# A block mask in an attention and mixer kernel: twelve wide matmuls and comparisons become one small group, one comparison and nine GpSimd copies, and the written order is new

## The chip, the cores and the metric

The kernel runs on one core of one Trainium2 chip. The core has five engines that work beside each other, each in its own order: TensorE (PE in the profile, its weight loads PEld), VectorE (DVE), ScalarE (ACT), GpSimd (POOL) and SyncE (SP), which here only issues DMAs. Each engine takes its instructions strictly in turn: one that waits holds up all behind it on that engine. The metric is the device time of one execution in microseconds (us), the median of three runs.

## The reference, cut to what matters

Attention with a block mask, and a mixer behind it. Batch 4, 8 heads, 768 tokens, 64 channels a head; the mask is made of blocks of 32 by 32, so 24 by 24 flags.

```python
scores = (1 / sqrt(64)) * q @ k.T
mask = |bi - bj| <= 1, or bi or bj in (0, 23), or bj in sampled_blocks[bi]   # bi, bj: block of row, column
attn = softmax(where(mask, scores, -1e9));  x = (attn @ v), heads side by side: [4, 768, 512]
u = x + (x.T @ U @ V).T                     # U [768, 32], V [32, 768]
out = u + relu(u @ w_ch1) @ w_ch2           # w_ch1 [512, 2048], w_ch2 [2048, 512]
```

## The kernel before

**Tiling.** The work on heads goes by pairs of heads: 16 pairs, four to a batch (`HP = 4`). A token is stored at partition p and position t as token 6p + t, so a tile of 128 partitions and 6 positions holds the 768 tokens, and a block of 32 tokens is a short stretch of partitions at each position. Scores are held transposed, keys on partitions, queries along the row; the exponential is taken without a maximum; the row of ones in `vts` makes the product with v give the sum too.

**Two ways to mask.** In the pairs 0 to 3 the mask sits in the matmul: beside the 64 channels of a head stand 24 rows, one-hot block numbers with the queries and block biases (0 or -240) with the keys, so that masked scores vanish in the exponential. From pair 4 on the queries and keys hold channels alone, two heads on the two halves of the array, and the exponentials are multiplied on VectorE by a tile `mask` of zeros and ones, 128 partitions by 6 key groups by 768 queries (`half_quad`, L990; the product is L1016). That tile has to be made once, before the first of these products. `mask_part` (L908) makes it: for each of 6 key groups and 2 halves of the queries one matmul of 24 meaningful rows (`kmask`, a zeroed tile into which a DMA, L197, copies the bias rows of the keys) against the one-hot rows, giving the bias of 128 keys for 384 queries, and one comparison on VectorE (L916) that turns it into zeros and ones.

**Steps and the written order.** A long string, `PLAN` (L436), lists the steps; each word is one step, and TensorE, VectorE, ScalarE and SyncE execute in the order in which the words issue their instructions. GpSimd isn't under that order: a scheduler of the framework places its instructions, by when it reckons them ready. A digit behind a word is the bank of PSUM (eight, numbered 0 to 7) that the step takes first. The words that matter here:

- `S` a score step of one key group in pairs 0 to 3, two matmuls of 384 columns; `B` one of two key groups, four matmuls, 1536 columns in three banks; `e` the exponential of the oldest score step not yet taken, on ScalarE. The 8 heads of pairs 0 to 3 have 48 key groups: here 30 `S` and 9 `B`, counted below as scores #1 to #48.
- `A` the product with v of one key group (6 matmuls of 65 columns), `v` the division on VectorE (L532, L539), `M`, `D`, `X`, `Y`, `E` steps of the low-rank mixer of pairs 0 to 3, with `m`, `d`, `y`, `g` their VectorE parts.
- `R` turns one half (queries or keys) of the next pair by six TensorE transposes (`turn_qk`, L921), and `t` copies it from PSUM on VectorE. `Z`, `z` do so for the second head of pair 0.
- `K` one `mask_part`, and `k` its comparison.
- `Q` a score step of both heads of a pair for two key groups (from pair 4 on; eight matmuls, L1001), `H` without dots one head of it; each gives two, or one, `e` of 1536 elements and as many `p`, the products with the mask. Below, Q4 is the first `Q` of pair 4, and so on. `V` is the product with v of one head.
- `U`, `P`, `C` and `a.`, `b`, `a` are the first mixer matmul and its relu, `H.`, `S.`, `D.` the second one in a scheme of seven products in place of eight, and `g.`, `h.` and what belongs to them the same for the last batch.

**Loads.** Queries, keys and values of pair i are loaded as float32 by SyncE (`load_qk`, `load_v`, L145 to L165), and cast to float16 on GpSimd (L139 for pairs up to 5). The load tiles and the cast tiles are doubled; the queue of SyncE stops at a load whose tile hasn't been cast away. `load_mix` (L199) brings U and V, cast on GpSimd too (L205, L206).

Of the kernel before, what the change touches and what calls it, by code (L numbers as in the profile page):

```python
# [19 lines left out]
P = 128  # L20
# [3 lines left out]
def kernel(  # L24
# [93 lines left out]
    kmask = consts.tile([P, S], FP16, name="kmask")  # L118
# [71 lines left out]
    for tile_ in (qres[1], kres[1], Vt, kmask):  # L190
        nc.gpsimd.memset(tile_.bitcast(FP32), 0.0)

    def second_set():
        for h in range(2):
            one_hot(1, h)
            nc.sync.dma_start(out=kres[1][mrows[h], h, :], in_=kres[0][mrows[h], h, :])
        nc.sync.dma_start(out=kmask[mrows[0], :], in_=kres[0][mrows[0], 0, :])  # L197
# [239 lines left out]
    S0 S3 e e S5 B0 e Z7 e S3 z Z6 e z B0 A7 A e R6 S3 t A R5 e A B0 t A K6 e A S3 k v A5 A e K6 k B0 A  # L437
    A e K7 A K6 k S3 k A K7 e v B0 k S3 e M6 e A5 A m R7 A t B0 K6 R3 e k A A t S6 A e v S0 D2 S3 e d A7
    A e A S0 K6 A e S3 k K2 A e S5 k A e v S3 R2 e S5 t S0 e M7 e S3 m D2 e B5 d A0 D1 e A A d A S3 D2 A
    e d K1 S5 k R7 e S3 t A S1 e v A5 A e A S3 S6 e K2 A e A k A S3 v B0 e K7 M6 e k S3 m X5 K7 e A6 Y k  # L440
    A B0 y X7 Y e S3 y E5 A e A g A R7 S0 t A e v S4 S2 e A7 A e R1 E6 A t A g A A Q v e e M6 X7 m Y P6
    y p H U7 e p H b C e p H b U7 e p H b U6 e p E1 a g p V7 Q v e e V6 U7 v p U0 a P1 b C p P6 a C E7 Q
    a g U6 e e U7 b P6 b p U0 C a U7 p a Q b X6 Y e e P7 y C P6 b C p U0 b a p V7 L.5 Q v U.0.1.3.6 e
    q.3.0 V7 a.0.1.3.0 e U.0.1.1.1 v U.0.1.11.0 a.0.1.1.1 U.0.1.5.6 q.3.1 a.0.1.11.1 p Q a.0.1.5.1 p
    U.0.1.10.6 e U.0.1.7.7 a.0.1.10.0 e U.0.1.2.6 a.0.1.7.0 S.0.0.1.3 U.0.1.9.7 p a.0.1.2.1 Q a.0.1.9.1
    q.7.1 U.0.1.4.6 e S.0.0.2.0 H.0.0.1.0.7 p H.0.0.1.1 a.0.1.4.1 U.0.1.0.0 p L.6 e U.0.1.14.1 q.4.1 V6
    a.0.1.0.1 p a.0.1.14.1 Q v q.4.0 e V6 D.0.0.0 S.0.0.3 H.0.0.6.0 e v U.0.1.13.2 q.7.0 H.0.0.6.1
    U.0.1.12.6 a.0.1.13.1 D.0.0.2 y p Q a.0.1.12.1 q.5.1 H.0.0.7.0 e H.0.0.7.1 q.5.0 H.0.0.5.0.6 D.0.0.3
    H.0.0.5.1 e S.0.0.4.4 U.0.1.6.1 p H.0.0.4.0 a.0.1.6.1 H.0.0.4.1 D.0.0.4 Q D.0.0.5 p H.0.0.3.0 e L.7
    H.0.0.3.1 p H.0.0.2.0.7 H.0.0.2.1 e p U.0.1.8.2 U.0.1.15.0 D.0.0.1 D.0.0.6 a.0.1.8.1 V7 p a.0.1.15.1  # L450
    S.0.1.1.1 Q S.0.2.1.0 V6 e v S.0.1.2.4 H.0.1.1.0.7 y v H.0.1.1.1 y H.0.1.2.0.0 S.0.2.2.3 y H.0.1.2.1
    e D.0.1.0 M6 D.0.1.1 H.0.2.1.0.1 m H.0.2.1.1 S.0.2.3 F.1.0.2.4 D.0.2.0 F.1.1.3.6 F.1.2.5.0 x.6.0
    H.0.2.6.0 x.6.1 d.6.0 H.0.2.6.1 x.7.0 d.6.1 F.1.3.6.4 D.0.2.2 H.0.1.6.0 T.6 x.5.1 H.0.1.6.1 S.0.1.3
    H.0.2.7.0 H.0.2.7.1 x.4.0 H.0.2.5.0.6 x.5.0 H.0.2.2.0.0 D.0.2.3 d.5.0 H.0.2.2.1 x.4.1 d.5.1
    H.0.2.4.0 D.0.1.2 d.4.0 T.5 x.7.1 H.0.2.4.1 d.7.0 H.0.1.7.0 D.0.2.1 d.4.1 D.0.2.5 H.0.1.7.1 d.7.1
    S.0.2.4.2 T.4 Q D.0.1.3 H.0.2.5.1 e H.0.1.4.0 T.7 D.0.2.4 H.0.1.4.1 H.0.2.3.0 e D.0.1.5 H.0.2.3.1
    Z.0.0.1 p H.0.1.5.0.7 Z.0.2.1 H.0.1.5.1 D.0.2.6 Q Z.0.2.0 D.0.1.4 Z.0.0.0 S.0.1.4.0 U.1.0.0.6 e
    H.0.1.3.0 a.1.0.0.0 H.0.1.3.1 e U.1.0.11.6 D.0.1.6 p U.1.0.10.0 Z.0.1.0 Z.0.1.1 a.1.0.11.1 U.1.0.9.7
    p L.8 a.1.0.10.1 U.1.0.6.6 a.1.0.9.1 p Q a.1.0.6.1 p U.1.0.12.6 e V7 e U.1.0.2.2 v U.1.0.5.0 p
    a.1.0.12.1 U.1.0.1.7 a.1.0.5.1 a.1.0.2.1 U.1.0.3.6 a.1.0.1.0 p Q a.1.0.3.1 V6 p e U.1.0.4.7 v e  # L460
    U.1.1.5.2 a.1.0.4.0 U.1.0.15.6 p a.1.1.5.1 U.1.1.9.7 a.1.0.15.1 p Q a.1.1.9.1 U.1.1.3.7 e L.9
    U.1.0.7.6 a.1.1.3.0 e U.1.0.14.7 a.1.0.7.0 p U.1.1.4.0 U.1.1.10.6 a.1.0.14.1 a.1.1.4.0 U.1.1.1.7 p
    a.1.1.10.1 Q a.1.1.1.1 V7 e V6 v e U.1.1.7.7 v Q a.1.1.7.1 p U.1.0.8.7 e H.1.0.1.0.6 a.1.0.8.0
    H.1.0.1.1 p e U.1.1.13.7 p U.1.0.13.0 U.1.1.14.2 p a.1.0.13.1 a.1.1.13.1 U.1.1.8.3 S.1.0.1.3
    a.1.1.14.1 U.1.1.6.7 a.1.1.8.1 S.1.0.3 Q a.1.1.6.1 S.1.0.2.0 H.1.0.2.0.7 e D.1.0.0 L.10 H.1.0.2.1
    S.1.0.4.4 H.1.0.6.0 D.1.0.1 H.1.0.6.1 e U.1.1.15.1 U.1.1.11.0 a.1.1.15.0 U.1.1.0.7 p a.1.1.11.1 Q
    D.1.0.2 a.1.1.0.1 p y V7 e H.1.0.7.0 v e H.1.0.7.1 U.1.1.2.0 p U.1.1.12.7 D.1.0.3 a.1.1.2.1 p Q
    a.1.1.12.1 S.1.1.1.0 H.1.0.4.0 e H.1.0.4.1 S.1.1.2.1 V7 D.1.0.5 e S.1.1.3 H.1.1.1.0.6 p H.1.1.1.1 Q
    D.1.1.0 v H.1.1.6.0 e L.11 p H.1.1.6.1 H.1.0.5.0.7 D.1.1.2 H.1.0.5.1 e p H.1.1.7.0 H.1.1.7.1 D.1.0.4
    V0 y p y y H.1.1.5.0.3 S.1.1.4.3 y V4 y D.1.1.3 v H.1.1.5.1 v y H.1.1.4.0 H.1.1.4.1 S.1.2.1.1 y  # L470
    H.1.0.3.0 D.1.1.4 M4 S.1.2.2.0 H.1.0.3.1 m D.1.1.5 F.2.0.5.4 F.2.1.0.1 D.1.0.6 Z.1.1.1 H.1.2.1.0.6
    x.8.0 H.1.2.1.1 x.10.0 d.8.0 H.1.1.3.0 x.10.1 d.10.0 F.2.2.7.5 D.1.2.0 F.2.3.4.2 d.10.1 H.1.2.2.0.1
    x.8.1 T.10 H.1.2.2.1 x.11.0 H.1.1.3.1 x.9.0 d.11.0 H.1.2.6.0 x.11.1 d.8.1 H.1.2.6.1 d.9.0 D.1.1.6
    T.8 H.1.1.2.0.7 D.1.2.1 d.11.1 x.9.1 H.1.1.2.1 S.1.2.3 d.9.1 Q T.11 D.1.2.2 D.1.1.1 e H.1.2.7.0
    H.1.2.7.1 T.9 H.1.2.5.0.7 D.1.2.3 e H.1.2.5.1 S.1.2.4.2 H.1.2.4.0 Z.1.1.0 H.1.2.4.1 Z.1.0.1 Q
    D.1.2.5 D.1.2.4 U.2.0.4.6 p e H.1.2.3.0 a.2.0.4.0 H.1.2.3.1 e U.2.0.12.6 D.1.2.6 U.2.0.5.7 Z.1.2.0
    Z.1.0.0 a.2.0.12.1 Q Z.1.2.1 a.2.0.5.0 p U.2.0.2.7 e L.12 U.2.1.8.6 a.2.0.2.0 U.2.1.1.7 a.2.1.8.1 e
    U.2.0.11.2 a.2.1.1.0 U.2.0.15.6 p a.2.0.11.1 U.2.0.0.7 p Q a.2.0.0.1 p a.2.0.15.1 U.2.0.9.7 e V6
    a.2.0.9.0 p e U.2.0.8.0 v U.2.0.10.7 a.2.0.8.1 U.2.1.4.6 a.2.0.10.0 p Q a.2.1.4.1 V7 p e U.2.1.0.6 v
    e U.2.0.13.1 a.2.1.0.0 U.2.0.1.7 p a.2.0.13.1 U.2.1.2.6 a.2.0.1.1 p Q a.2.1.2.0 U.2.1.9.7 e L.13  # L480
    U.2.0.7.6 a.2.1.9.0 e U.2.0.6.7 a.2.0.7.0 p U.2.0.14.6 a.2.0.6.1 q.0.1 Q a.2.0.14.1 p V7 e q.0.0 V6
    v e q.1.1 U.2.0.3.7 v Q a.2.0.3.1 p H.2.0.1.0.7 e p U.2.1.5.6 H.2.0.1.1 S.2.0.1.4 e U.2.1.10.0
    a.2.1.5.0 U.2.1.14.1 S.2.0.2.1 a.2.1.10.0 U.2.1.3.6 a.2.1.14.1 D.2.0.0 Q S.2.0.3 a.2.1.3.1 p
    H.2.0.6.0 e H.2.0.2.0.6 p H.2.0.6.1 H.2.0.2.1 e D.2.0.2 U.2.1.13.0 D.2.0.1 S.2.0.4.3 H.2.0.7.0
    a.2.1.13.1 H.2.0.7.1 p y Q p V6 e D.2.0.3 H.2.0.4.0 v e H.2.0.4.1 V6 D.2.0.5 p Q v U.2.1.11.7 e
    H.2.0.5.0.6 a.2.1.11.0 H.2.0.5.1 q.1.0 e U.2.1.12.7 p U.2.1.15.0 p a.2.1.12.1 U.2.1.7.1 a.2.1.15.1
# [676 lines left out]
```

## Time and profile before

| what | us |
|---|---|
| time, three runs | 274.45 median (274.29 to 274.58) |
| span of the profiled execution, first to last instruction | 271.1 |
| TensorE busy in the span | 261.9 (97%) |
| VectorE busy | 235.3 (87%) |
| ScalarE busy | 202.5 (75%) |
| GpSimd busy | 84.7 (31%) |
| 12 mask matmuls (L910) busy | 3.9 |
| 12 mask comparisons (L916) busy | 6.5 |

The profiled execution has no time of its own beside its span; against the median of the runs, 3.35 us lie outside the span. A matmul's end is modelled, so a busy TensorE isn't TensorE at its peak: the distance from one matmul's start to the next's tells more than its busy time. Four stretches can be told apart by the starts of score steps: up to 6.8 us the first loads; 6.8 to 43.4 pairs 0 to 3, where the mask is made; 43.4 to about 224 pairs 4 to 15 together with the mixer of the batches before; and from there the mixer of the last batch.

### The profile page before, as it was taken

The numbers are of one execution on the slowest core, as the hardware profiler recorded it, in microseconds if no ns is written. First come the engines' busy times: TensorE is split into PE (matmuls) and PEld (weight loads), VectorE is DVE, ScalarE is ACT, GpSimd is POOL, SyncE is SP. The second block draws the span as 40 slices with busy tenths as digits, with TensorE's granted clock in tenths as the row PEclk, the third lists the DMA queues.
The fourth block names the chain that finished last, engine by engine and source line by source line (L and its number), as shares of the span: only waits on it lengthen the run. The fifth ranks groups of instructions, "written<-read, shape, count | busy, mean of one in ns | idle before, by whom it ended". The sixth has DMA issues, their size and how long they took to land.

```text
span 271.1 us, 7373 instructions
## 1 busy us (share of the span) xinstructions
PE 261.9 (97%) x3008; PEld 182.1 (67%) x3008; DVE 235.3 (87%) x475; ACT 202.5 (75%) x264; POOL 84.7 (31%) x164
## 2 busy tenths in 40 slices
PE   7899999999999999999999999999999999999993
PEld 3577776555567778565666877565667788657882
DVE  5699988988999998868688997688998999999992
ACT  3889998897989666788888847788997943889100
POOL 4479104931628643035624660044000000000000
PEclk9999999999999999999999999999999999999998
DMA  5799997999974664872527356670200116300024
GB/s 161 239 305 316 199 210 173 225 131 198 155 222 67 201 204 91 278 217 59 178 45 190 64 212 117 221 208 16 46 0 2 41 41 142 134 0 0 22 78 136
DMA packets 49698, 37.58 MB, mean 139 GB/s; under 512 B 30528, under 2 KB 46816, under 8 KB 49664
## 3 DMA queue, kind: packets, MB, share of 16 engines
q1 hardware_dynamic: 46688, 32.67, 45.9%
q0 software_dynamic: 2688, 4.19, 10.9%
q8 instruction: 23, 0.38, 0.6%
q10 hardware_dynamic: 288, 0.24, 0.3%
q14 instruction: 11, 0.09, 0.1%
HBM read 27.67 MB, written 6.29 MB: 125 GB/s over the span
## 4 chain that ended last, share of the span: by engine, by line
PE 72%; DVE 17%; DMA 4%; ACT 2%; issue 1%; SPq 1%; POOL 0%; DVEq 0%; ACTq 0%
PE ps L748 28%; PE ps L673 20%; PE ps L402 9%; PE ps L1001 8%; DVE est L1016 5%; DMA qld<-in_q_dram 3%; PE ps L951 2%; DVE xf L867 2%; DVE xf L539 2%; DVE sums L843 1%; DVE res L709 1%; DMA vld<-in_v_dram 1%; ACT est L1010 1%; PE ps L970 1%; DVE sums L709 1%
## 5 line engine op out<-in xcount | busy, mean ns | idle before, releaser
L1010 ACT ACTIVATE est<-ps 128x1536 f16<-128x1536 f32 x72 | 100.6, 1450 | 18.9 <-PE ps L1001 18.9
L673 PE MATMUL ps<-uT,w1t 128*128 128x384 f16 x384 | 70.2, 326 | 0.2 <-DVE hid L687 0.2
L1016 DVE TENSOR_TENSOR est<-est,mask 128x1440 f16<-128x1440 f16 x72 | 65.5, 933 | 0.2
L673 PEld LDWEIGHTS <-w1t 128*128 128x128 f16 x384 | 35.6, 98 | 26.9 <-issue 7.0
L402 PEld LDWEIGHTS <-est 128*128 128x128 f16 x1152 | 40.2, 97 | 7.2 <-ACT hid L685 1.3
L402 PE MATMUL ps<-vt,est 128*128 128x65 f16 x1152 | 43.3, 193 | 0.1
L142 POOL CAST stqld<-qld 128x192 f16<-128x192 f32 x40 | 19.9, 540 | 73.2 <-DMA qld<-in_q_dram 36.0
L748 PEld LDWEIGHTS <-hid 128*128 128x128 f16 x360 | 34.3, 98 | 7.0 <-issue 1.9
L685 ACT ACTIVATE hid<-ps 128x384 f16<-128x384 f32 x63 | 29.7, 495 | 4.7 <-PE ps L673 4.3
L1001 PE MATMUL ps<-qpl,kpl 64*128 64x512 f16 (+1 forms) x288 | 31.6, 325 | 0.0
L748 PE MATMUL ps<-w2t,hid 128*128 128x256 f16 x240 | 31.3, 273 | 0.2 <-DVE xf L539 0.2
L867 DVE TENSOR_TENSOR xf<-xf,ps 128x256 f32<-128x256 f32 x63 | 25.0, 411 | 3.7 <-PE ps L748 3.3
L687 DVE TENSOR_SCALAR hid<-ps 128x384 f16<-128x384 f32 x33 | 18.2, 553 | 8.1 <-PE ps L673 7.5
L748 PEld LDWEIGHTS <-sums 128*128 128x128 f16 x216 | 20.3, 98 | 4.7 <-issue 1.1
L142 POOL CAST stkld<-kld 128x192 f16<-128x192 f32 x40 | 22.3, 597 | 2.5 <-DMA kld<-in_k_dram 2.5
L960 ACT ACTIVATE est<-ps 128x768 f16<-128x768 f32 x30 | 22.5, 813 | 0.6 <-PE ps L951 0.6
L1001 PEld LDWEIGHTS <-kpl 64*128 64x128 f16 x288 | 12.1, 94 | 14.3 <-issue 9.1
L748 PE MATMUL ps<-res,sums 128*128 128x256 f16 x144 | 19.4, 273 | 0.3 <-DVE xf L867 0.3
L622 ACT CAST xh<-xf 128x384 f16<-128x384 f32 x24 | 11.0, 510 | 10.4 <-DVE xf L618 10.4
L539 DVE TENSOR_TENSOR xf<-ps,rcp 128x384 f32<-128x384 f32 x32 | 17.7, 553 | 0.8
L142 POOL CAST vt<-vld 128x192 f16<-128x192 f32 x40 | 17.9, 487 | 0.0
L748 PE MATMUL ps<-res,hid 128*128 128x256 f16 x120 | 15.9, 273 | 0.0
(121 smaller groups left out, 341.5 us busy)
## 6 DMA issues: line engine op xcount, KB each, us to landing
vld<-in_v_dram SPq DMA_DIRECT2D x16, 384.0 KB, 4.6
qld<-in_q_dram SPq DMA_DIRECT2D x15, 384.0 KB, 3.5
kld<-in_k_dram SPq DMA_DIRECT2D x15, 384.0 KB, 5.5
out_dram<-xf SPq DMA_DIRECT2D x18, 256.0 KB, 2.2
w1t<-in_moe_w_ch_dram POOLq DMA_DIRECT2D x4, 512.0 KB, 8.2
w2t<-in_moe_w_ch_dram POOLq DMA_DIRECT2D x4, 512.0 KB, 10.4
out_dram<-xf SPq DMA_DIRECT2D x12, 128.0 KB, 1.7
qld<-in_q_dram SPq DMA_DIRECT2D x2, 192.0 KB
```

The lines of the kernel that those rows point to most:

```text
L142: last = nc.gpsimd.tensor_copy(out=dst[:, h, ts], in_=ld[:, h, ts])
L402: nc.tensor.matmul(pav[:, sc, :], est[:, n, sc * P : (sc + 1) * P], vts[b % 2][:, 2 * hp + h, g, 0 : D + 1], start=(g == 0 and sc == 0), s ...
L539: nc.vector.tensor_tensor(out=dst, in0=pav[:, :, 0:D], in1=rcp[:, :, None].broadcast_to([P, T, D]), op=ALU.mult,)
L673: nc.tensor.matmul(pt, w1t[:, cc, jj * P : (jj + 1) * P], bts[b].uT[:, cc, c * HS : (c + 1) * HS], start=(cc == 0), stop=(cc == NCC - 1), ...
L685: nc.scalar.activation(out=dst, in_=pt, func=AF.Relu)
L687: nc.vector.tensor_scalar_max(out=dst, in0=pt, scalar1=0.0)
L748: nc.tensor.matmul(acc[key], lhsT, rhs, start=(first and i == 0), stop=(i == len(pairs_) - 1), skip_group_check=True,)
L867: nc.vector.tensor_add(out=x, in0=x, in1=acc[a, b, tau])
L960: lambda: nc.scalar.activation(out=dst, in_=ps, func=AF.Exp, scale=0.125),
L1001: nc.tensor.matmul(units[h][:, u * S + lo : u * S + hi], kT[drows[h], g * P : (g + 1) * P], qT[drows[h], lo:hi], start=True, stop=True, sk ...
L1010: nc.scalar.activation(out=both[h], in_=units[h].rearrange("p (g n) -> p g n", g=2), func=AF.Exp, scale=0.125,)
L1016: lambda: nc.vector.tensor_mul(out=masked(both[h]), in0=masked(both[h]), in1=masked(mask[:, 2 * j : 2 * j + 2, :]),),
```

## The change

The tile `kmask`, its clearing on GpSimd and the DMA that filled it are gone. In place of twelve `mask_part` there is one `mask_flags`: six matmuls of 24 columns, one for each key group, put the bias of 128 keys for each of 24 query blocks in one bank, and one comparison of 128 by 144 elements makes `flags`. Three `mask_spread` then repeat the flags along the queries on GpSimd: since a token is 6p + t, the queries of one block aren't a rectangle of the tile, and each third of the blocks takes one large copy and some small ones. The calls make nine copies in all: three large (1440, 1152 and 1440 elements of a partition) and six small (96 each).

The list of steps is another one throughout. Apart from the mask, every engine gets the same instructions, as many of each kind; their order on an engine differs in places.

```diff
-    kmask = consts.tile([P, S], FP16, name="kmask")
+    flags = consts.tile([P, T, NB], FP16, name="flags")
...
-    for tile_ in (qres[1], kres[1], Vt, kmask):
+    for tile_ in (qres[1], kres[1], Vt):
         nc.gpsimd.memset(tile_.bitcast(FP32), 0.0)
...
-        nc.sync.dma_start(out=kmask[mrows[0], :], in_=kres[0][mrows[0], 0, :])
...
-    S0 S3 e e S5 B0 e Z7 e S3 z Z6 e z B0 A7 A e R6 S3 t A R5 e A B0 t A K6 e A S3 k v A5 A e K6 k B0 A
-    A e K7 A K6 k S3 k A K7 e v B0 k S3 e M6 e A5 A m R7 A t B0 K6 R3 e k A A t S6 A e v S0 D2 S3 e d A7
+    S0 Z7 e S4 e S0 e B3 e Z2 z z K0 k S6 e B1 e S4 e R7 R6 t t B0 S4 e e A7 A A A A A B1 J A6 A A A A A S4
+    e e B0 e v v M3 m A5 A A S3 e R7 B0 R4 t t S6 A A A v e S3 e e A2 A D0 d S6 e S3 e R5 t S6 S0 A A A A v
+    e e S6 S4 e e S0 e M3 m D2 S3 B5 D0 d D2 d d e e A1 A A A A S3 e A v S6 e R0 S3 A5 A S6 e e A A J J t S1
...
-    def mask_part(g, c, n):
-        pm = bank(n, [P, HS], FP32)
-        nc.tensor.matmul(
-            pm, kmask[:, g * P : (g + 1) * P], qres[0][:, 0, c * HS : (c + 1) * HS],
-            start=True, stop=True,
-        )
+    def mask_flags(n):
+        pm = bank(n, [P, T, NB], FP32)
+        for g in range(T):
+            nc.tensor.matmul(
+                pm[:, g, :], qres[0][mrows[1], 1, g * P : (g + 1) * P], bias[0:NB, 0, 0:NB],
+                start=(g == 0), stop=(g == T - 1), skip_group_check=True,
+            )
         then(
             "k",
             lambda: nc.vector.tensor_single_scalar(
-                out=mask[:, g, c * HS : (c + 1) * HS], in_=pm, scalar=-1.0, op=ALU.is_ge
+                out=flags, in_=pm, scalar=-1.0, op=ALU.is_ge
             ),
         )
+    def mask_spread(r):
+        per = 3 * BLK // T
+        to = mask.rearrange("p g (t b i) -> p g t b i", t=T, i=per)
+        of = flags.rearrange("p g (b r) -> p g b r", r=3)[:, :, None, :, r, None]
+        runs = {}
+        for t in range(T):
+            inside = [i for i in range(per) if (T * i + t) // BLK == r]
+            runs.setdefault((inside[0], inside[-1] + 1), []).append(t)
+        lo, hi = max(i for i, _ in runs), min(i for _, i in runs)
+        pieces = [(lo, hi, range(T))]
+        for (i0, i1), ts in runs.items():
+            pieces += [(i, j_, ts) for i, j_ in ((i0, lo), (hi, i1)) if i < j_]
+        for i0, i1, ts in pieces:
+            dst = to[:, :, ts[0] : ts[-1] + 1, :, i0:i1]
+            nc.gpsimd.tensor_copy(out=dst, in_=of.broadcast_to(dst.shape))
...
-        "K": ((mask_part, g, c) for g, c in each(range(T), (0, 1))),
+        "K": ((mask_flags,) for _ in range(1)),
+        "J": ((mask_spread, j) for j in range(3)),
```

In the built program GpSimd's queue holds, behind the casts of pair 1's queries and keys: a copy of 1440, one of 96, one of 1152, one of 96; the cast of pair 1's values, the cast of U; three copies of 96, one of 1440; the cast of V, the cast of pair 2's queries, one copy of 96, the cast of pair 2's keys; from there on as before. Before, the five casts stand there alone, in the same order.

## The prediction

> **What bounds the kernel now.** I read the page's shares first, then the windows cut at the score steps, then in each stretch the idle times of the engines and the timeline. TensorE is at 97% on the page, but its ends are modelled, so where it really bounds has to come from idle times and from starts. The window of pairs 0 to 3, the one behind it, and the waits of that first window:
>
> ```profile
> 6.80:43.40 36.60, 34.93 (x502) 25.95 (x500) 31.48 (x69) 34.18 (x39) 17.65 (x24) 1.00 1.00 251
> 52.80:66.20 13.40, 13.40 (x156) 8.21 (x154) 11.84 (x21) 10.83 (x13) 3.71 (x8) 1.00 1.57 151
> ```
>
> (length; then busy time of PE, PEld, DVE, ACT, POOL; granted clock; DMA share; GB/s.)
>
> ```profile
> ACT est L978 <- PE ps L970: 1.5, 6, 0.4
> ACT est L1010 <- PE ps L1001: 1.2, 1, 1.2
> ACT est L960 <- PE ps L951: 0.6, 1, 0.6
> ```
>
> From the first exponential at 7.33 to the end of the last of pairs 0 to 3 at 43.06, ScalarE is idle for only 2.1 us (1.5 + 0.6); another 1.2 pass before the first exponential of pair 4. Ten exponentials of 768 run in 7.24 us, 0.72 each; one of 1536 takes 1.34 from start to start; 30 x 0.72 + 9 x 1.34 = 33.7 of the 35.7 us. So ScalarE bounds this stretch. DVE has 36.60 - 31.48 = 5.1 us to spare there.
>
> Later TensorE bounds. Between Q5 (52.80) and Q15 (203.27) lie 30 Q, 87 full groups of the first mixer matmul, 92 of the second, 19 V and a few small steps. By the start-to-start times of the chain (0.76 for a Q, 0.65, 0.435, 1.09) that is 22.8 + 56.6 + 40.0 + 20.7 + 3.3 = 143.4 of 150.5 us: TensorE has 7.1 us of gaps in all, half a us in a pair's stretch. The end has none:
>
> ```profile
> 224.14 41.68 PE ps L748 x326
> ```
>
> (chain of waits: start, length, what.) What the reader should keep: a us that TensorE or ScalarE loses before 43 us has no place to come back.
>
> GpSimd is idle most of the time, but not from 14 to 28 us, where it casts the loads of pairs 1 to 4 (start, length, what, idle before it):
>
> ```profile
> 11.40 0.83 POOL L139 CAST stkld<-kld 128x768 f16<-128x768 f32 x1 [0.17 <-DMA kld<-in_k_dram]
> 14.09 0.83 POOL L139 CAST vt<-vld 128x768 f16<-128x768 f32 x1 [1.86 <-DMA vld<-in_v_dram]
> 14.86 0.35 POOL L205 CAST Ut<-uld 128x192 f16<-128x192 f32 x1
> 15.41 1.57 POOL L206 CAST Vt<-vld 32x768 f16<-32x768 f32 x1 [0.20 <-DMA vld<-in_moe_V_dram]
> 17.30 0.83 POOL L139 CAST stqld<-qld 128x768 f16<-128x768 f32 x1 [0.33 <-PE ps L402]
> 18.30 0.82 POOL L139 CAST stkld<-kld 128x768 f16<-128x768 f32 x1 [0.16 <-PE ps L910]
> ```
>
> The cast at 17.30 is pair 2's queries, done at 18.13; TensorE turns them at 19.80, only 1.7 us later. Right behind stand B of scores #19 and #20, and the exponential that waits for it:
>
> ```profile
> 19.80 0.50 PE L924 MATMUL ps<-small,stqld 128*128 128x128 f16 x6
> 20.49 0.81 PE L970 MATMUL ps<-res 128*128 128x512 f16 x4
> ```
>
> ```profile
> 21.40 1.45 ACT L978 ACTIVATE est<-ps 128x1536 f16<-128x1536 f32 x1 [0.26 <-PE ps L970]
> ```
>
> **The change, part by part.** *TensorE.* Twelve matmuls of 384 columns go: 0.16 each in the chain, 2.0 us. Six of 24 columns come: between 0.03 (36 of 65 columns in 1.09) and 0.057 (6 of 128 columns in 0.34) each, so 0.2 to 0.35; I take 0.3. Net -1.7 us, all before 43 us, where ScalarE's exponentials cover it: worth 0. Without that cover it would be -1.7.
>
> *VectorE.* Twelve comparisons go, three in 1.56, about 6.0 us. One of 144 elements comes; nearest is the 128x128 copy at 0.28. Net -5.7, under the same cover and in an engine with 5.1 to spare: 0 by itself.
>
> *SyncE.* The kmask DMA leaves, which held the queue from 10.05 to 10.82. The loads behind it (pair 1's values, U, V, pair 2) go out 0.77 earlier. GpSimd waited 1.86 for the first of them, but will now be busy with copies then: 0. The cleared kmask (0.42) lay before a wait of 2.97: 0.
>
> *GpSimd.* Nine copies come, and this is what the forecast turns on. Four of them (1440, 96, 1152, 96 elements) stand right behind the cast that ends at 12.23. Their flags are there by then: the new K needs banks freed by exponentials #3 and by Z, about 10 us, and its comparison ends near 11. Then come pair 1's values, U, three small copies, the last large one, V, and only then pair 2's queries. The trace shows no float16 copy that repeats its input. Lower bound: the casts in long runs, (833 - 350) / (768 - 192) = 0.84 ns an element and 0.19 fixed. Upper: the V cast, which reads every sixth element, (1.57 - 0.19) / 768 = 1.8 ns. I take 1.0 ns: the copies read few bytes again and again, and write in runs of 4 or 5, nearer to the long runs than to an element here and there; the short runs I let cost a fifth. So from 12.23, in us:
>
> 1. Four copies: 3.1 at the low price, 3.6 at mine, 5.8 at the high one: 15.3, 15.8, 18.0.
> 2. Pair 1's values 0.77, U 0.45: 16.6, 17.0, 19.2.
> 3. Three small copies and the large one: 2.2, 2.5, 3.9: 18.8, 19.5, 23.1.
> 4. V 1.57, pair 2's queries 0.33 + 0.83: 21.5, 22.2, 25.8, in place of 18.1.
>
> In the new list pair 2's first R stands where it stood, behind score #18, with B of #19 and #20 right behind it. TensorE reaches it near 19.7. It then waits for the cast, turns (0.34), and B follows; in the trace 0.91 pass from B's start to its exponential. That gives exponentials #19 and #20 at 22.8, 23.5, 27.1, against 21.40: +1.4, +2.1, +5.7. Nothing else fills ScalarE: #18 is its last score by then. The second R needs pair 2's keys, a small copy and a cast later (about 1.3), which is shorter than R and B: nothing more. The casts of pairs 3 and 4 slide with it (SyncE's loads too, since they wait for cast tiles), but pair 3's first R stands behind #24, some 3 us of exponentials later, and its cast about 2.3 behind pair 2's. The weights w1, issued behind pair 3's keys, took 5.7 to 12.9 us to land from 22.7 to 25.2, and are first used at 45.4: covered, even 6 us later.
>
> *Given back before 43 us.* From 22.75 to 43.06 ScalarE's idle time is 0.5. At the end, three scores stand together and both R of pair 4 come before the last four A, so the 1.2 before pair 4's first exponential may shrink to about 0.85. I count 0.5 in all, between 0 and 0.9. Net at Q4: +0.9, **+1.6**, +5.2.
>
> *The new order behind Q4.* Counts are the same between Q5 and Q15 and behind. It moves relus, sums and halves of products past each other, and lets some stores go ahead of transposes in SyncE's queue; none leaves a step without its input that I can see. The gain is bounded by the 7.1 us of gaps, the loss by nothing that a row shows, but by symmetry I put it at no more than 2. I take -0.5.
>
> Sum: +1.6 - 0.5 = +1.1. The profiled span of 271.1 would become 272.2, and the median, 3.35 outside the span, **275.6**.
>
> [...] The row: reading every sixth float32 costs 1.57 us where the dense cast of as many elements costs 0.83. [...]
>
> **The rivals.** (1) *The forecast*: a stall of 1.5 to 3.5 us at pair 2's first R: 275.0 to 278.0.
>
> (2) *The copies go at the dense price*, so that only +0.9 is left at Q4: 274.45 + 0.9 - 0.5 = 274.9, within 0.2%. For it: the copies' reads stay within a few bytes. Against it: the short runs of the writes. [...]
>
> (3) *The copies go like the V cast*, or worse: +5.2 - 0.5, 279.2. For it: that cast is the only one that doesn't run along memory. Against it: its step is 24 bytes, here 0 or 6.
>
> (4) *Faster: the new order closes gaps of TensorE behind Q4.* There are 7.1 us; closing half gives +1.6 - 3.5, 272.6. It decides from 2.2 us on (1.6 + 0.55). For it: the order of the halves of products is now free (second before first in places), and around the joints of batches the chain runs over VectorE for some us (69.7 to 73, 212.5 to 221). Against it: in 52.80 to 66.20 the profile shows no idle TensorE at all.
>
> (5) *The change doesn't remove work from any bound*: -1.7 on TensorE would only count if ScalarE weren't the cover; 274.45 + 1.1 - 1.7 = 273.9. ScalarE's 33.7 of 35.7 speak against it, and I count it with (4).
>
> **How the numbers follow.** What a measurement of this kernel can tell from no change is about 0.2%, 0.55 us. Chances: (1) 0.45, (2) 0.15, (3) 0.12, (4) and (5) 0.28. So faster 0.28, same 0.15, slower 0.57. The likeliest case alone reaches from 275.0 to 278.0. The range has to reach into (4) and to (3): 273.0 to 279.2 leaves out about a tenth at the fast end and less at the slow end.
>
> **What would show it.** In the trace after: GpSimd's copies start at 12.2, the large ones taking 1.2 to 1.8 us (0.2 to 0.4 the small ones); pair 2's queries are cast at about 21 to 22; TensorE waits at R for that cast, and ScalarE is idle for 2 us or more just before the exponential of #19. If the cast ends before 20, (1) is wrong, and if the large copies take 2.3 us or more, (3) is right. Q4's first matmul should come at 45 (43.4 before), and the distance from there to the end should be 226 to 228 us, as now (227.7): if it is under 225.5, (4) has happened, above 229 the new order costs. I'd be wrong most easily in the price of a copy, which counts nearly four times over, and in the half us given to the new order, which stands on no row.

## The result, and the profile after

The changed kernel takes 277.13 us (median of nine runs, 275.87 to 279.12) beside 274.58 for the kernel before (nine runs on the same chip, 272.86 to 275.99). The ratio is 1.010, with a 95% interval of 1.0066 to 1.0134: slower by about 2.6 us. The forecast was 275.6, with 275.0 to 278.0 for its own case. So the side was right and the size too small. The profiled execution has a span of 274.1 us, 3.0 more than before.

Single executions of either kernel differ by up to 3.25 us. Each kernel here has one profiled execution, and in the twelve of them the first exponential comes anywhere from 7.16 to 9.12 us, so up to 2 us of that can lie ahead of it, where the change hardly matters yet (more on that at the end). Below, stretches are therefore counted from the first exponential of the execution: to Q4 (the first score step of pair 4), and from Q4 to the end of the span.

| from the profiled executions, us | before | after | difference |
|---|---|---|---|
| start of the first exponential | 7.33 | 7.58 | +0.25 |
| from there to the exponential of scores #19 and #20 | 14.07 | 15.21 | +1.14 |
| first exponential to Q4 | 36.07 | 37.19 | +1.12 |
| Q4 to the end | 227.70 | 229.33 | +1.63 |

The same windows of busy time as before, now cut at the changed kernel's own steps (up to Q4, from 0.25 later to match the later start; Q5 to the first step of pair 6), with the columns as in the prediction:

```profile
7.05:44.77 37.72, 34.34 (x497) 24.59 (x496) 26.37 (x58) 34.25 (x39) 22.74 (x31) 1.00 0.93 235
54.23:67.60 13.37, 13.37 (x154) 8.11 (x151) 12.86 (x23) 10.80 (x13) 7.52 (x15) 1.00 1.21 221
```

VectorE's 31.48 us have become 26.37, and GpSimd went from 17.65 to 22.74. TensorE's 34.93 have become only 34.34, in a stretch that is 1.12 longer; its ends are modelled. ScalarE is as busy as before (34.18, now 34.25), but the stretch is a us longer. Its waits for the B steps in this stretch say why; before, they (then L970, now L984) were 1.5 us in six pieces of at most 0.4:

```profile
ACT est L992 <- PE ps L984: 2.6, 3, 2.1
```

One wait of 2.1 us is new; the other two for B steps make 0.5 together. The timeline of TensorE and of ScalarE around it:

```profile
21.54 0.51 PE L938 MATMUL ps<-small,stqld 128*128 128x128 f16 x6 [1.87 <-POOL stqld L139]
21.88 0.81 PE L984 MATMUL ps<-res 128*128 128x512 f16 x4
...
22.79 1.45 ACT L992 ACTIVATE est<-ps 128x1536 f16<-128x1536 f32 x1 [2.15 <-PE ps L984]
```

TensorE stands 1.87 us at the transposes of pair 2's queries (L938) and waits for GpSimd's cast of them (`stqld`, L139). The scores #19 and #20 are right behind, and ScalarE waits for those. GpSimd's timeline shows what the cast stood behind:

```profile
12.12 3.54 POOL L933 COPY mask<-flags 128x1440 f16<-128x1440 f16 x4
15.29 1.02 POOL L139 CAST vt<-vld 128x768 f16<-128x768 f32 x1
16.25 0.35 POOL L204 CAST Ut<-uld 128x192 f16<-128x192 f32 x1
16.55 2.67 POOL L933 COPY mask<-flags 128x96 f16<-128x96 f16 x4
19.18 1.53 POOL L205 CAST Vt<-vld 32x768 f16<-32x768 f32 x1
20.66 0.82 POOL L139 CAST stqld<-qld 128x768 f16<-128x768 f32 x1
```

The first four copies (1440, 96, 1152 and 96 elements; the row carries the shape of the first) hold the queue from 12.12 to 15.29, the next four from 16.55 to 19.18. The queries are cast at 20.66 to 21.48; before, that cast ended at 18.13.

The last stretch, the row of the chain of waits that answers to the 41.68 us of before, is without a break again (start, length, what):

```profile
227.72 42.85 PE ps L743 x336
```

**Behind Q4** most distances from one score step to the next are the same within 0.2 us. The others lie in four stretches, which take, from end to end:

| stretch | before | after |
|---|---|---|
| third step of pair 6 to second of pair 8 | 30.87 | 31.45 |
| first step of pair 11 to third of pair 12 | 30.18 | 30.99 |
| first step of pair 13 to first of pair 14 | 12.73 | 13.89 |
| first step of pair 15 to the end | 67.83 | 67.12 |

The timeline of after at the three places that became longer, first TensorE's rows, then VectorE's, then SyncE's queue; below it SyncE's queue of before at the third place:

```profile
80.99 0.54 PE L401 MATMUL ps<-vt,est 128*128 128x65 f16 x12 [0.51 <-DVE est L1030]
173.19 0.48 PE L668 MATMUL ps<-uT,w1t 128*128 128x384 f16 x2 [0.75 <-DMA uT<-xh]
188.30 2.76 PE L668 MATMUL ps<-uT,w1t 128*128 128x384 f16 x16 [0.89 <-DVE xf L534]
...
187.69 0.56 DVE L534 TENSOR_TENSOR xf<-ps,rcp 128x384 f32<-128x384 f32 x1 [1.53 <-DMA out_dram<-xf]
...
165.18 5.47 SPq L606 DMA_TRANSPOSE uT<-xh  x4
175.03 1.33 SPq L690 DMA_DIRECT2D out_dram<-xf  x3
176.72 1.26 SPq L374 DMA_TRANSPOSE qpl<-stqld  x1
178.08 1.23 SPq L374 DMA_TRANSPOSE kpl<-stkld  x1
179.36 0.57 SPq L150 DMA_DIRECT2D qld<-in_q_dram  x1
179.98 0.46 SPq L150 DMA_DIRECT2D kld<-in_k_dram  x1
180.49 0.47 SPq L161 DMA_DIRECT2D vld<-in_v_dram  x1
181.00 1.41 SPq L690 DMA_DIRECT2D out_dram<-xf  x3
```

```profile
168.55 5.19 SPq L695 DMA_DIRECT2D out_dram<-xf  x5
174.12 1.25 SPq L375 DMA_TRANSPOSE qpl<-stqld  x1
```

- At 80.99 the product of pair 6 with v waits for a mask product on VectorE; weight sums (`q`) stand ahead of it there in the new list. The step from pair 6 to pair 7 takes 5.60 us for 4.91.
- At 173.19 the mixer waits for a transposed tile `uT`. The four transposes of that group (`T` in the list) are issued in another order: pair 10's, which is used first, is now the last of four.
- At 188.30 the mixer waits for VectorE, which at 187.69 waits for a store. The division of pair 12 (batch 3) writes the tile `xf`, of which there are two, so it reuses the one of batch 1 and must wait until that batch's last stores have landed. Three of them stand behind two transposes and the three loads of pair 15 in SyncE's queue, and go out at 181.00. Before, all of batch 1's stores went out ahead of those, the last five from 168.55 on.

The chain of waits has the third place on it, with the store's landing:

```profile
181.00 0.47 SPq L690
...
181.98 5.62 DMA out_dram<-xf
```

### The profile page after: what moved, and what is told of

Same layout as the page of the kernel before. It is cut to its first block, busy times and chain, and to the rows that moved or that the text cites. A ratio compares the mean times of both kernels' runs of the same rounds, so it can differ in the third digit from the quotient of the medians.

```text
span 274.1 us, 7363 instructions
## 1 busy us (share of the span) xinstructions
PE 262.4 (96%) x3002; PEld 180.1 (66%) x3002; DVE 230.1 (84%) x464; ACT 202.5 (74%) x264; POOL 84.7 (31%) x172
## 4 chain that ended last, share of the span: by engine, by line
PE 69%; DVE 13%; DMA 7%; POOL 3%; ACT 3%; SPq 2%; issue 2%; ACTq 0%; DVEq 0%
PE ps L743 28%; PE ps L668 19%; PE ps L401 9%; PE ps L1015 8%; DMA kld<-in_k_dram 4%; DVE est L1030 3%; DMA out_dram<-xf 2%; PE ps L965 2%; POOL mask L933 2%; DVE xf L534 2%; DMA uT<-xh 1%; DVE xf L862 1%; ACT est L992 1%; ACT xh L617 1%; SPq L374 1%
## 5 line engine op out<-in xcount | busy, mean ns | idle before, releaser
L1030 DVE TENSOR_TENSOR est<-est,mask 128x1440 f16<-128x1440 f16 x72 | 64.5, 926 | 0.5 <-ACT est L1024 0.4
L401 PEld LDWEIGHTS <-est 128*128 128x128 f16 x1152 | 38.7, 97 | 7.0 <-issue 1.6
L401 PE MATMUL ps<-vt,est 128*128 128x65 f16 x1152 | 41.1, 193 | 0.7 <-DVE est L1030 0.5
L743 PE MATMUL ps<-w2t,hid 128*128 128x256 f16 x240 | 32.2, 273 | 0.1
L142 POOL CAST stkld<-kld 128x192 f16<-128x192 f32 x40 | 18.9, 513 | 1.6 <-DMA kld<-in_k_dram 1.3
L142 POOL CAST vt<-vld 128x192 f16<-128x192 f32 x40 | 16.3, 448 | 0.6 <-DMA vld<-in_v_dram 0.6
```

Of the source, the lines that this page charges most:

```text
L142: last = nc.gpsimd.tensor_copy(out=dst[:, h, ts], in_=ld[:, h, ts])
L401: nc.tensor.matmul(pav[:, sc, :], est[:, n, sc * P : (sc + 1) * P], vts[b % 2][:, 2 * hp + h, g, 0 : D + 1], start=(g == 0 and sc == 0), s ...
L743: nc.tensor.matmul(acc[key], lhsT, rhs, start=(first and i == 0), stop=(i == len(pairs_) - 1), skip_group_check=True,)
L1030: lambda: nc.vector.tensor_mul(out=masked(both[h]), in0=masked(both[h]), in1=masked(mask[:, 2 * j : 2 * j + 2, :]),),
```

## The experiments

The theory: the loss is two things that have nothing to do with each other. (A) GpSimd's copies hold up the cast of pair 2's queries, ahead of Q4. (B) The new written order puts three DMAs or sums in worse places behind Q4, the stores above all. Rivals: the loss behind Q4 follows from the stall (a shifted pipeline), or from the new mask, and not from the list; and the removal of TensorE's and VectorE's mask work is worth something that the stall hides.

Ratios are to the kernel before in the same set of runs (its medians there were 274.59, 274.70 and 274.54). Where an expectation speaks of seven mask copies, it is the nine that the program has; where one speaks of the loads of pair 13, it is those of pair 15, which the word `L.12` issues. Stretches come from one profiled execution of each kernel.

**Late copies, in the new list.** The nine GpSimd copies are held until the values of pair 4 are cast.

```diff
-        cast(i, vts[b % 2][:, 2 * hp : 2 * hp + 2, :, 0:D], ld)
+        v_cast[i] = cast(i, vts[b % 2][:, 2 * hp : 2 * hp + 2, :, 0:D], ld)
...
-            nc.gpsimd.tensor_copy(out=dst, in_=of.broadcast_to(dst.shape))
+            with tc.issue_after(v_cast[HP].ins):
+                nc.gpsimd.tensor_copy(out=dst, in_=of.broadcast_to(dst.shape))
```

> The changed kernel, but the nine mask copies are queued on GpSimd behind the cast of pair 4's values (about 30 us), where GpSimd is idle until 42. Theory (two causes: the copies in front of pair 2's casts, and the new order behind Q4): pair 2's queries are cast by 18.5, TensorE doesn't wait at their turning, the exponential of scores #19 and #20 starts at 21.0 to 21.5 (22.79 in the changed kernel) and Q4 comes 1.1 to 1.6 earlier, at 43.2 to 43.7 (44.77); the distance from Q4 to the end stays at 229.3, so the time is 275.5 to 276.0 and still above the kernel before. Rival (the copies were harmless, ScalarE had lost the time to something else, such as the loads that come later): Q4 stays at 44.5 or later and the time at 277.1. Rival (everything is the stall): 274.5.

275.49 us, ratio 1.003 (0.9992 to 1.0069). GpSimd's and ScalarE's timeline of this kernel:

```profile
16.43 0.82 POOL L140 CAST stqld<-qld 128x768 f16<-128x768 f32 x1
...
28.02 6.60 POOL L935 COPY mask<-flags 128x1440 f16<-128x1440 f16 x9
...
21.04 1.45 ACT L994 ACTIVATE est<-ps 128x1536 f16<-128x1536 f32 x1 [0.26 <-PE ps L986]
```

The queries are cast at 16.43, the nine copies run in a row at 28.02, when nobody waits for GpSimd, and the wait of 2.15 us before the exponential is 0.26 again. The first exponential to Q4 takes 35.28 us instead of 37.19: the copies cost 1.91 there. Q4 to the end stays at 229.62, so the loss behind Q4 does not come from the stall. The experiments below have nearly the same steps ahead of Q4, and give the spread of the 1.91: 37.43 and 37.76 in two more executions with early copies, 35.16 to 35.48 in four more with late ones. TensorE's wait for the cast of pair 2's queries is 2.35 in one of the former and 1.03 in the other. The one of 1.03 has the longer start (see the end): its first exponential comes 1.4 us later than in the changed kernel.

**Old list with the new mask, and the same with late copies.** The list of before, with one `K`, its `k`, and three `J` in place of the twelve `K` and `k`; beside it the same kernel with the edit of the first experiment.

```diff
-    S0 Z7 e S4 e S0 e B3 e Z2 z z K0 k S6 e B1 e S4 e R7 R6 t t B0 S4 e e A7 A A A A A B1 J A6 A A A A A S4
+    S0 S3 e e S5 B0 e Z7 e S3 z Z6 e z K6 k B0 A7 A e R6 S3 t A R5 e A B0 t A e A S3 v A5 A e B0 J J J A A e
...
```

> The new mask (one matmul group, one comparison, nine copies) under the step list of the kernel before: its twelve K and k are gone, one K and k stand behind the second Z, and the three spreads behind scores #13 and #14. GpSimd's queue holds the copies at nearly the place that they have in the changed kernel. Theory of two causes: the exponential of #19 and #20 at 22.4 to 23.2, Q4 at 44.3 to 45.0, and from Q4 to the end 227.5 to 228 as in the kernel before; time 275.5 to 276.0 (ratio 1.003 to 1.006). Rival (the copies alone cost everything): 277. Rival (the mask change by itself gains, and the new list alone costs): 273 to 274.5.

> As the last one, with the copies behind the cast of pair 4's values. Nothing of the kernel before is left worse, 1.7 us of matmuls and 5.7 us of comparisons are gone. Theory (ScalarE bounds pairs 0 to 3, so the removed work lay under cover): exponential of #19 and #20 at 21.0 to 21.4, Q4 at 42.9 to 43.4, time 274.0 to 274.6, no more than 0.5 below the kernel before. Rival (the removed work lay on the path): Q4 at 41.5 to 42.3 and the time at 272.5 to 273.3.

Early copies: 275.19 us, ratio 1.0021 (0.9989 to 1.0053). Late copies: 274.99, ratio 1.0012 (0.9978 to 1.0047). The times alone can't tell these two apart; the profiled executions can. First exponential to Q4: 37.61 us with early copies, 36.03 with late ones, 36.07 in the kernel before. So the copies cost 1.58 in this list, and without the stall the twelve removed matmuls and comparisons are worth nothing that shows (0.04, where executions of the same steps differ by 0.3). The medians differ by 0.2 only, and both times miss what was expected, by 0.3 downward and 0.4 upward. Q4 to the end is 228.21 and 228.65, 0.5 to 0.9 above the kernel before and 0.7 to 1.1 below the changed one: about half of the loss of 1.63 behind Q4 goes with the list. The rest is left with the old list too, most of it at pair 7, of which more below.

**Stores ahead of the loads.** The changed kernel with three words moved.

```diff
-    ... q.0.1 Z.1.0.1 Z.1.2.1 Q L.12 e e ... Q e e Z.1.1.1 Z.1.0.0 Z.1.1.0 v y V6 ...
+    ... q.0.1 Z.1.0.1 Z.1.2.1 Q Z.1.1.1 Z.1.0.0 Z.1.1.0 L.12 e e ... Q e e v y V6 ...
```

> The changed kernel with three steps of its list moved: the last three stores of batch 1's output stand ahead of the transposes and loads that come before Q13, as in the kernel before, not behind them. Theory (the division of pair 12 waits 1.5 us for these stores, because batch 3's output tile takes batch 1's place): the wait of VectorE for the stores is gone, TensorE's 0.89 before the first mixer matmuls of that stretch too, and Q13 to Q14 takes 12.7 to 12.9 in place of 13.89; Q4 to the end 228.1 to 228.3, time 275.9 to 276.2. Rival (the stretch is bound by VectorE's new order, and the wait only shows where): Q13 to Q14 stays at 13.5 or more, the time at 277.

276.02 us, ratio 1.0051 (1.0021 to 1.0080). The stretch from pair 13 to pair 14 is 12.73 us again (13.89 in the changed kernel), and no step of TensorE waits there. The place costs 1.16 and its cause is shown: with the three stores ahead of the loads nothing waits for them. Q4 to the end is 227.55, 1.78 less; the rest came around pairs 6 to 8 (30.56 instead of 31.45 from the third step of pair 6 to the second of pair 8), a place that this edit does not touch, of which more below.

**Both edits together.**

> The changed kernel with both repairs: the seven mask copies wait for the cast of pair 4's values, and the three stores of batch 1 stand ahead of three loads of pair 13's in SyncE's queue. If the stall and the stores are two separate causes that add, the first exponential to the first step of pair 4 takes 35.3 us (as with the late copies alone) and pair 4 to the end 227.6 to 228.1, together 263.0 to 263.4 against 263.8 of the kernel before, and the time is 0.3 to 0.9 us below the kernel before: ratio 0.997 to 0.999. If the store wait only moves to another tile when the stage ahead is shorter, pair 4 to the end stays at 229 and the time is level or above the kernel before.

274.69 us, ratio 0.9998 (0.9961 to 1.0035). First exponential to Q4 35.16, Q4 to the end 228.03: 263.19 together, against 263.77 before and 266.52 after. Against the changed kernel that is 2.0 less ahead of Q4 and 1.3 less behind it (1.9 and 1.8 by the edits alone): two causes at two places, each with its own repair, and with both gone the kernel is where it was before the change. The stretches are nearly as expected, the median is not: 0.3 to 0.9 below the kernel before was expected, and it is level.

**The transpose and the weight sums, in the changed kernel.** `T.10` behind the cast of its own input, and the sums of experts 7 and 5 behind the products that pair 6's values wait for.

```diff
-    ... x.10.1 d.10.1 x.8.1 d.8.1 T.8 ... Q e e T.10 U.2.0.4.6 ...
+    ... x.10.1 d.10.1 T.10 x.8.1 d.8.1 T.8 ... Q e e U.2.0.4.6 ...
-    q.7.0 q.4.0 q.4.1 p p q.5.1 p V6 D.0.0.0 p L.6 Q e e H.0.0.6.0 v q.5.0
+    p p q.4.0 q.4.1 p V6 D.0.0.0 p L.6 Q e e H.0.0.6.0 v q.7.0 q.5.1 q.5.0
```

> The changed kernel with only those two places put back (pair 10's transpose first of its group, the weight sums of experts 7 and 5 behind the mask products), copies and stores left as in the change. By the comparison of the traces pair 4 to the end falls from 229.33 to 228.1 and the time by 1.2 us against the changed kernel, to 275.0 to 276.0 (ratio 1.002 to 1.006). If they are worth nothing, it stays at 229.3 and the ratio at about 1.01.

276.54 us, ratio 1.0070 (1.0032 to 1.0107): a miss, above the 275.0 to 276.0 expected. Both places did by themselves what the comparison of the traces had promised: pair 6 to 7 fell from 5.60 to 4.91, the second to third step of pair 12 from 4.62 to 3.70. But Q4 to the end fell only by 0.35, to 228.98. Most of the rest was given back at two next waits. One is the next step, pair 7's first to second, 4.78 instead of 4.42. The other is the store, by this kernel's timeline of VectorE and TensorE:

```profile
187.39 0.56 DVE L534 TENSOR_TENSOR xf<-ps,rcp 128x384 f32<-128x384 f32 x1 [2.01 <-DMA out_dram<-xf]
...
188.00 2.76 PE L668 MATMUL ps<-uT,w1t 128*128 128x384 f16 x16 [1.36 <-DVE xf L534]
```

VectorE now waits 2.01 us for the store (1.53 in the changed kernel) and TensorE 1.36 (0.89). The store, which lands at a time set by SyncE's queue, took back 0.47 of what TensorE had gained ahead of it.

**All four places, and all but the weight sums.** Late copies, stores ahead of the loads and `T.10` early, with the weight sums moved and without.

> Both repairs, and two more places of the new list put back as they were: the transpose of pair 10 issued first of the four of its group, and the weight sums of experts 7 and 5 behind the mask products that pair 6's values wait for. If each of these places costs what the comparison of the two traces shows, the step from the second part of pair 6 to pair 7 falls from 5.60 to about 5.0 us, the step from the second to the third part of pair 12 from 4.62 to about 4.0, pair 4 to the end is 226.5 to 227.0, and the ratio is 0.993 to 0.997. If TensorE's next wait takes their place, pair 4 to the end stays at 227.6 to 228.1 and the ratio at that of the kernel with the two repairs.

> Late copies, the three stores ahead of the loads, and pair 10's transpose first of its group, in the new list; the weight sums stay as in the change. If moving the weight sums only moved a wait from one V to the next (the kernel with all four edits had 5.60 fall to 4.90 at one and 4.42 rise to 5.32 at the next), this one is as fast as that: first exponential to pair 4 35.2 to 35.5, pair 4 to the end 227.1 to 227.6, ratio 0.993 to 0.997. If the weight sums were worth something, it is 0.3 to 0.7 us slower than the kernel with all four.

With the sums moved 273.34 us, ratio 0.9952 (0.9915 to 0.9989); without, 273.19 us, ratio 0.9941 (0.9906 to 0.9976). By their medians both are faster than both kernels. The second to third step of pair 12 is 3.70 and 3.71, and with the stores early no store takes that back. The medians fall by 1.35 and 1.50 against the kernel with two edits, more than the 0.9 that the place had cost, but within what the intervals leave open. The profiled executions don't show this gain: Q4 to the end is 228.27 with the sums moved (226.5 to 227.0 expected) and 227.70 without (227.1 to 227.6 expected), against 228.03 with two edits. From the first exponential to the end that makes 263.75 and 262.99, against 263.19 with two edits and 263.77 before. How much of the 0.5% comes from the transpose is therefore open. Moving the sums bought nothing: pair 6 to 7 fell to 4.90 and pair 7's first to second step rose to 5.32, and from the third step of pair 6 to the second of pair 8 it is 31.32 with them moved and 31.34 without.

**New list up to Q4, old list behind it.** With late copies.

```diff
-    ... A7 A R3 t R4 t A A A A v Q e M6 X7 m Y y P6 p e p H U7 ...
+    ... A7 A R3 t R4 t A A A A Q v e e M6 X7 m Y P6 y p H U7 e ...
```

> The new list up to the first step of pair 4, the old list from there on, the new mask, and the seven GpSimd copies that can wait held behind the cast of pair 4's values. If the new order behind pair 4 is a cost of its own, as I now hold, the first exponential to pair 4 takes 35.2 us (as with the late copies in the new list) and pair 4 to the end 227.7 to 228.3 (as with the old list throughout), together 262.9 to 263.5 against 263.8 of the kernel before: a time of 273.6 to 274.4, ratio 0.996 to 0.999. If the stores, the transposes and the weight sums of the new tail were answering something that the new head or the GpSimd mask brings, pair 4 to the end stays near 229.5, as with the late copies in the whole new list, and the ratio at 1.003.

273.39 us, ratio 0.9972 (0.9934 to 1.0009). First exponential to Q4 35.16, as expected, and the ratio is the one expected of the first case. Q4 to the end is 228.70, though, between the two expectations: behind pair 8 no step takes over 0.15 longer than before, so the places of the transpose and the stores are gone, but TensorE waits 0.99 us at pair 7, where this list is word for word that of before. This is the place that moved in nearly every experiment. The timeline of the kernel before there, VectorE and then GpSimd:

```profile
76.60 1.72 DVE L1016 TENSOR_TENSOR est<-est,mask 128x1440 f16<-128x1440 f16 x2
78.23 0.68 DVE L709 TENSOR_TENSOR res<-w2t,res 128x1024 f16<-128x1024 f16 x1
78.83 0.90 DVE L1016 TENSOR_TENSOR est<-est,mask 128x1440 f16<-128x1440 f16 x1
...
80.37 2.21 POOL L142 CAST stqld<-qld 128x192 f16<-128x192 f32 x4 [4.84 <-issue]
```

And of the kernel with the old tail, VectorE, GpSimd, TensorE:

```profile
76.02 2.01 DVE L1032 TENSOR_TENSOR est<-est,mask 128x1440 f16<-128x1440 f16 x2
77.95 0.82 DVE L705 TENSOR_TENSOR res<-w2t,res 128x1024 f16<-128x1024 f16 x1
78.70 1.04 DVE L1032 TENSOR_TENSOR est<-est,mask 128x1440 f16<-128x1440 f16 x1
...
74.76 3.47 POOL L143 CAST stkld<-kld 128x192 f16<-128x192 f32 x4
78.18 2.35 POOL L143 CAST vt<-vld 128x192 f16<-128x192 f32 x4
...
80.50 1.26 PE L402 MATMUL ps<-vt,est 128*128 128x65 f16 x36 [0.99 <-DVE xf L535]
```

VectorE does the same instructions in the same order in both. In the kernel before, GpSimd is idle from 75.5 to 80.37, and two mask products take 1.72, a third 0.90, a weight sum 0.68. In the other, GpSimd casts through the whole stretch, the products take 2.01 and 1.04 and the sum 0.82. VectorE falls behind by 0.14 with each, and TensorE waits 0.99 for its division. The slowing itself holds over the whole traces of before and after: 87 mask products that ran while GpSimd did nothing took 0.90 to 0.91 us each, and 38 that ran beside it for more than nine tenths of their time took 0.89 to 1.07, 26 of them over 0.93. The weight sums took 0.68 to 0.69 alone (66 of them) and 0.68 to 0.84 beside it (32, of which 29 over 0.71). The divisions into `xf` took 0.55 to 0.56 either way (29 and 27); why they differ from the others no run shows.

That this slowing makes TensorE wait at pair 7 is only suggested by the rows, and isolated by no run; what the rows shown lose adds up to 0.57, less than the 0.99. The place varies without any edit there: from the third step of pair 6 to the second of pair 8 it took 30.56 to 31.50 us in the six kernels with the new list that leave it as it is. But the kernel before stands apart: from the third step of pair 6 to the second of pair 7 GpSimd is busy for 4.4 us and the stretch takes 9.22, while in the eleven others GpSimd is busy for 6.5 to 8.0 and the stretch takes 9.45 to 10.22. With one profiled execution of the kernel before, it is open whether that is chance or goes with the new mask.

**Each copy issued twice**, in the changed kernel.

```diff
-            nc.gpsimd.tensor_copy(out=dst, in_=of.broadcast_to(dst.shape))
+            for _ in range(2):
+                nc.gpsimd.tensor_copy(out=dst, in_=of.broadcast_to(dst.shape))
```

> The changed kernel with each of the seven mask copies issued twice, nothing else. GpSimd's work ahead of the cast of pair 2's queries grows by the copies that stand ahead of it, 3.54 + 2.67 = 6.2 us by the changed kernel's timeline. If GpSimd's queue is the whole of the stall, that cast ends at about 27.7 instead of 21.5, the exponential of scores 19 and 20 starts about 6.2 us later than in the changed kernel against the first one, and pair 4 starts 5 to 6 us later (part is given back). If the stall comes from something else (the comparison, the small matmul group), pair 4 moves by under 2 us.

280.28 us, ratio 1.0204 (1.0128 to 1.0279). The place of the loss was missed. Nobody writes GpSimd's order here; the framework's scheduler placed the cast of pair 2's queries ahead of most of the doubled copies, and #19's exponential came 14.48 us behind the first one (15.21 in the changed kernel), a little earlier, not 6 later, in an execution with the longer start. The other copies then stood before the later casts, and the wait went with them: TensorE waits 0.76 for the cast of pair 2's queries, and 1.91 for that of pair 3's, where the changed kernel doesn't wait. Counted from the first exponential, Q4 came 1.12 us later than in the changed kernel, and Q4 to the end grew by 1.41, of which 1.51 is at pair 5's second step, behind a weight sum that waits for a cast of GpSimd (1.6 us). So the run doesn't test the stall at #19 as it was meant to; it shows that the doubled copies were paid for at the casts that the scheduler happened to put behind them.

## Why the prediction came out as it did

| term | forecast | measured |
|---|---|---|
| removed TensorE and VectorE mask work | 0 | -0.04 (old list, late copies: 36.03 against 36.07) |
| stall through the copies | +2.1 | +1.91 (new list), +1.58 (old list) |
| new list ahead of Q4, "given back" | -0.5 | -0.8 (late copies: 35.28 against 36.07) |
| net at Q4 | +1.6 | +1.12 |
| new order behind Q4 | **-0.5** | **+1.63** |
| sum | +1.1 | +2.75, and +0.25 of a later start: the span's +3.0 |

**What bounds the stretch up to Q4** was right. ScalarE's exponentials set its length, and VectorE's 5.1 us less and the twelve matmuls less moved nothing that shows. Rival (5) falls with it.

**The stall** was right in its place, cause and nearly its size. TensorE waits at the transposes of pair 2's queries for GpSimd's cast, ScalarE for the scores behind. The cast ended at 21.48; the three ways of pricing had given 21.5, 22.2 and 25.8. The first four copies took 3.17 from start to start (3.1, 3.6 and 5.8 had been worked out), the other four 2.63 (2.2, 2.5, 3.9), and V with the queries behind it 2.30 instead of 2.73, since the pause before the cast is gone. So the eight copies took 5.80, between the dense price (5.3) and the forecast's own (6.1), and nearer to the latter; the cast ended where the dense price had put it because V and the queries took 0.43 less. One price an element fits no better: a copy of 1440 took 1.37 to the next one's start and the other 1.60 (1.40 by the dense price, 1.63 with the fifth added for short runs), the one of 1152 took 1.38 (1.16 and 1.34). Rival (3) falls. Rival (2) had the end of the cast right but not the time, because its other term was the one that failed. From start to start the large copies, which read in steps of 0 and 6 bytes, took 0.95 to 1.20 ns an element, and the V cast, in steps of 24 bytes, 1.9 (1.49 us for 768); whether the step makes the difference no run isolates.

**Given back ahead of Q4**: the size is near, the place is not. The prediction looked for it between #20 and Q4, and there the changed kernel takes 21.98 us from #19's exponential to Q4, against 22.00 before. The gain lies ahead of #19: with late copies the first exponential to #19 takes 13.44 instead of 14.07, and ScalarE's waits for the B steps up to #19 are 0.46 us instead of 1.20. In the changed kernel that leaves +1.14 at #19, where +2.1 had been forecast, and nothing given back behind it.

**The step that failed** is "The new order behind Q4", the -0.5 that "stands on no row". Its own sentence held the mistake: "lets some stores go ahead of transposes in SyncE's queue; none leaves a step without its input that I can see". It names the stores that go ahead and not the three that fall behind, and it asks for inputs alone. The store is not an input of anything: it is what frees the tile `xf` for the division of the next batch but one, and it went behind three loads, 1.16 us in the stretch. The other term was an order of inputs, `T.10`, last of its group of four instead of first: 0.81 over its stretch; put back, the last step of that stretch fell by 0.92. Both stand in the lists: for each DMA that moved past another, one can ask who waits for it. The remaining 0.58 at pairs 6 to 8 isn't pinned on an edit: moving the weight sums didn't bring it back, and the rows only suggest VectorE's slower products beside GpSimd's casts. The prediction's sum of gaps, 7.1 us from Q5 to Q15, is 0.7 for each of ten pairs, not half a us. The loss stayed inside the bound of 2 that was set for it; the middle of a range without a row was taken as a value, and its sign was wrong.

That the time still fell into the range of the forecast's own case, 275.0 to 278.0, is partly luck. That case was a stall alone; with the +1.12 measured at Q4 and the -0.5 it would have been 275.1, at the lower edge. More than half of the loss in the profiled span lies behind Q4, where a gain was counted on.

Rival (4), that the new order closes gaps behind Q4, got its 0.7 us at the end (pair 15 to the end, 67.83 to 67.12) and lost more than it elsewhere. What was to show it worked as written: Q4 came at 44.77 (45 forecast), copies started at 12.12 (12.2), the large ones took 1.43 to 1.64 (1.2 to 1.8), and Q4 to the end was 229.33, past the 229 from which "the new order costs". The small copies showed 0.6 to 0.8 each in the trace where 0.2 to 0.4 was written; from start to start they took 0.2 to 0.4.

The median was 3.35 above the profiled span before, and the prediction put that "outside the span". In the runs with both numbers the time is 1.8 above the span (275.87 and 274.1 after); by that the profiled execution of before would have had a time of 272.9, 1.5 below its median. That fits the two starts described below: of the eleven other profiled executions, the seven with the shorter start lie 0.0 to 2.0 below their kernel's median, the four with the longer one between 0.5 below and 0.9 above.

## What to carry to other kernels

- Work taken from covered engines bought nothing here (0.04 us ahead of Q4), and the same work put on an idle engine cost what it delayed in that engine's queue (1.91). Ask first what stands behind it in the next 10 us. Here the same copies, issued 16 us later, cost nothing that shows ahead of Q4.
- When a written order changes, go through what each moved DMA frees as well as what it feeds: here stores behind loads held up the division that reuses their tile, by 1.53 us. And repair the last of such waits first, since it can take back what is gained ahead of it, as here, where TensorE's wait went from 0.89 to 1.36.
- A term without a row should enter a sum as a range with both signs, not as its pleasant half.

## What the runs showed of the hardware

- **The start has two lengths, and TensorE's first instructions go with them.** In four of the twelve profiled executions the first six transposes took 0.84 to 0.85 us, the first matmul of 384 columns behind them 0.50, and the first exponential came at 8.65 to 9.12; in seven they took 0.52 and 0.33 and it came at 7.16 to 7.71 (in one, 0.71, 0.33 and 7.34). The transposes start at 4.96 to 5.51 in both cases. The windows don't show whether the granted clock differs: they read 1.00 in all twelve from 0 to 5 us and from 5 to 9.2, but so does a stretch ahead of the clock's record, which begins at 3.44 us in before and at 4.05 in after. Why some executions start slower no run here shows. It moves the first exponential by 0.9 to 2.0 us, as much as the effects studied here, which is why stretches were counted from there. In the kernel with the stores moved ScalarE waits for TensorE for another 0.88 us behind the first exponential, where the changed kernel doesn't wait, so its 37.43 to Q4 still holds a part of the slow start.
- **Three stores took 5.5 to 5.6 us to land** behind three loads of 384 KB in their queue (after, issued from 181.00 on). The three of the same batch that went out ahead of those loads, at 175.03, took 2.3 to 2.7, and in the kernel before, where all six did, 2.0 to 2.3. The median of such stores on the page is 2.2 (before) and 2.5 (after).
- **The price of a repeating copy on GpSimd does not go by elements.** From start to start in the changed kernel 1440 elements took 1.37 us (the second time 1.60), 1152 took 1.38, and 96 took 0.21 or 0.41. In the program the 1440 and the 1152 are both 288 runs, of 5 and of 4. No run separates the two readings, by elements and by runs.
- **VectorE's mask products and weight sums took 16 and 21% longer beside GpSimd's casts** in the rows shown above: 0.90 against 1.04, 0.68 against 0.82. In the traces of before and after 12 of the 38 products and 3 of the 32 sums beside GpSimd were not slowed, nor was any of the 27 divisions.
